# Pooled attention and two dense layers: keys and values of two heads laid out as one run of 144 groups

## The chip, the cores and the metric

One core of a Trainium2 chip runs the whole program. The metric is the time of one execution on the device in microseconds (us). The median of the runs shown is compared, and a profiled execution of the same kernel says where the time lies.

## What is computed

The inputs q, k and v have 8 batches, 8 heads, 576 positions and 64 elements each, in float32. Keys and values are averaged over groups of 8 neighbouring positions, so that a head has 72 pooled keys and 72 pooled values. What follows is the reference, cut to its core:

```
k_p = k.reshape(B, H, Sp, 8, D).mean(axis=3)
v_p = v.reshape(B, H, Sp, 8, D).mean(axis=3)
scores = scale * q @ k_p.T
attn = exp(scores - max(scores)); attn = attn / (sum(attn) + 1e-9)
x = (attn @ v_p) as 4608 tokens x 512
h = x @ w_in;  x = max(0.01 * h, h) @ w_out          # 512 -> 2048 -> 512
h = x @ w_in2; out = max(h, 0) ** 2 @ w_out2         # 512 -> 2048 -> 512
```

## The kernel before

The program runs through three stages that overlap. Attention goes batch by batch and writes its result to a scratch tensor in DRAM; the first layer pair works on the tokens that are ready; from some 500 us on attention is over, and the two layer pairs alone are left. The change lies in attention alone.

**Batch 0** is written out by hand in `first_batch`: a fixed order of loads, pooling, scores, softmax, transposes and output products, mixed with the first weight loads (`fetch`) and their decoding (`w`). `in_order` (L94) ties every instruction of it to the one before on its engine. **Batches 1 to 7** are a generator; the loop over the layer pair's units calls `advance()` to draw a piece of attention between two units, by a count and not by time. In this part the framework orders each engine's work itself, so that an engine may do a piece well before the source's place.

**Loads.** All loads of q, k, v and weights, and the stores of attention, are issued by SyncE (its queue is SPq in the profile) one after the other; only the first half of batch 0's keys goes through ScalarE's queue. A head's 72 groups of 8 positions (a group is one row of 512 values, 2 KB) are cut into 64 and 8. `load_main` (L378, issue on L386) loads the 64: for each of four pairs of heads two transfers of 64 rows (128 KB) each, one to partitions 0 to 63 and one to 64 to 127, so eight for a tensor of a batch. `load_rest` (L392, issue on L395) loads the last 8 groups of all eight heads, 64 rows, in one transfer. Keys and values take turns in the same buffers.

**Keys**, `prepare_k` (L422): `pooled` (L351, instructions on L356) adds the 8 positions of each row in three VectorE steps of 256, 128 and 64 values a row (times the number of pairs). Its last step writes `kd`. In batch 1 TensorE sums instead (`pooled_pe`, L359). The rest's sums go to `rr` and are copied beside themselves (L428). Two TensorE transposes turn `kd` (L440 in batch 0, L448 later), one turns `rr` (L451), all into one PSUM tile `trk`; four ScalarE instructions (L456 and L460, for each half) put the turned keys into `kT`, which is zero elsewhere, so that a matmul yields the scores of two heads at once (L554).

**Values**, `prepare_v` (L464): pooled in the same way into `vd`; two ScalarE and two VectorE instructions (L500, L501), each on 64 partitions, write the high and low parts into `vM`, where a zero block keeps the two heads of a pair apart. The rest's values are multiplied by a block mask on GpSimd (L474), moved by six small SyncE transfers to `rx` (L482), and become `vR`.

**Softmax**, `stage_parts` (L542): for each of 40 chunks of up to 128 tokens VectorE takes the maxima, ScalarE the exponentials (L571) and VectorE the sums' reciprocals (L584). GpSimd multiplies: L586 the first 64 columns of each head (512 values) and twice L593 the last 8 columns of four heads, each three times over (96 values). TensorE transposes the result (L604 and L616), ScalarE and VectorE split it (L605, L606, L617, L619), and `stage_d` multiplies with `vM` and `vR` (L317 to L319 and L638, tile `o`).

PSUM tiles of this part come from `work` (L122), a ring of four banks that transposes, scores, `o` and the layers' `h` share. The core of the parts in question:

```
issue[m // 2].dma_start(out=ts[-1][a * KM:(a + 1) * KM, m % 2],
    in_=src[b, heads[m][a], 0:KM * POOL, :].rearrange("(kk j) d -> kk (j d)", j=POOL))
...
nc.gpsimd.tensor_tensor(
    out=pp[:n, 0:DM].rearrange("p (h x) -> p h x", x=KM), in0=x[:n, :, 0:KM],
    in1=rs[:n].to_broadcast([n, H, KM]), op=ALU.mult)
```

Of the kernel before, what the change touches and what calls it, by code (L numbers as in the profile page):

```python
# [19 lines left out]
KM = 64  # L20
# [7 lines left out]
def raw(ap):  # L28

    return ap.bitcast(F32)  # L30
# [3 lines left out]
def attention_two_mlps(  # L34
# [17 lines left out]
    KR = SP - KM  # L52
    NP = H // 2
    NK = DM // P
    NF = DFF // P
    RG = KR * H // 2
# [265 lines left out]
    def attention():  # L322

        with ExitStack() as s:
# [6 lines left out]

            mask = one.tile([KR * H, H, D], F32, name="mask")
            nc.gpsimd.memset(mask, 1.0 / POOL)
            nc.gpsimd.affine_select(
                out=mask, in_=mask, compare_op=ALU.is_ge, fill=0.0, base=0,
                pattern=[[-KR, H], [0, D]], channel_multiplier=1,
            )
            nc.gpsimd.affine_select(
                out=mask, in_=mask, compare_op=ALU.is_ge, fill=0.0, base=KR - 1,
                pattern=[[KR, H], [0, D]], channel_multiplier=-1,  # L340
# [12 lines left out]
            def pooled(dst, src):  # L353

                for n in (POOL * D // 2, POOL * D // 4, D):
                    nc.vector.tensor_tensor(  # L356
                        out=dst if n == D else src[:, :, 0:n], in0=src[:, :, 0:n], in1=src[:, :, n:2 * n], op=ALU.add
                    )

# [11 lines left out]
            def kv_tile(b, rows, n, name):  # L371

                if b == 0:
                    t = w_late.tile([rows, 2, POOL * D], F32, tag="w", name=name)
                    return t[:, 0:n]
                return kvp.tile([rows, n, POOL * D], F32, tag=f"kv{n}", name=name, bufs=n)

            def load_main(b, src, nm, heads, issue=None):  # L378

                issue = issue or [nc.sync, nc.sync]  # L380
                ts = []
                for m in range(NP):
                    if m % 2 == 0:
                        ts.append(kv_tile(b, P, 2, f"{nm}{b}_{m}"))
                    for a in range(2):
                        issue[m // 2].dma_start(  # L386
                            out=ts[-1][a * KM:(a + 1) * KM, m % 2],
                            in_=src[b, heads[m][a], 0:KM * POOL, :].rearrange("(kk j) d -> kk (j d)", j=POOL),
                        )
                return ts  # L390

            def load_rest(b, src, nm, issue=None):  # L392

                t = kv_tile(b, KR * H, 1, f"r{nm}{b}")
                (issue or nc.sync).dma_start(  # L395
                    out=t[:, 0], in_=src[b, :, KM * POOL:S, :].rearrange("h (kk j) d -> h kk (j d)", j=POOL)
                )
                return t


# [3 lines left out]
            def load_k(b):  # L404
                if b < B:
                    both = [nc.scalar, nc.sync] if b == 0 else [nc.sync, nc.sync]
                    KV["k", b] = (
                        load_rest(b, k, "k", both[1]),
                        load_main(
                            b, k, "k", [[4 * (m // 2) + m % 2 + 2 * a for a in range(2)] for m in range(NP)], both  # L410
                        ),
                    )

            def load_v(b):
                KV["v", b] = (
                    load_rest(b, v, "v"),
                    load_main(b, v, "v", [[2 * m, 2 * m + 1] for m in range(NP)]),
                )

            def prepare_k(b):  # L422
                kr, kk = KV.pop(("k", b))
                i = b % 2
                kd = ap1.tile([P, NP, D], F32, tag="kd", name=f"kd{b}")
                rr = ap1.tile([KR * H, 2, D], F32, tag="rr", name=f"rr{b}")
                pooled(rr[:, 0:1], kr)
                nc.vector.tensor_copy(rr[:, 1], rr[:, 0])  # L428
                if b in K_ON_PE:
                    for ps in pooled_pe(f"kp{b}", kk):  # L430
                        yield
                    nc.scalar.copy(kd, ps)
                else:
                    for m in range(0, NP, 2):
                        pooled(kd[:, m:m + 2], kk[m // 2])
                        if b > 0:
                            yield
                            continue
                        tr = work("trk0") if m == 0 else tr
                        nc.tensor.transpose(  # L440
                            tr[:, m * D:(m + 2) * D], kd[:, m:m + 2].rearrange("p a d -> p (a d)"), ident
                        )
# [4 lines left out]
                for g in range(2 if b > 0 else 0):  # L447
                    nc.tensor.transpose(  # L448
                        tr[:, g * P:(g + 1) * P], kd[:, 2 * g:2 * g + 2].rearrange("p a d -> p (a d)"), ident
                    )  # L450
                nc.tensor.transpose(  # L451
                    tr[:, 2 * P:2 * P + KR * H], rr.rearrange("p a d -> p (a d)"), ident[:KR * H, :KR * H]
                )
                for r in range(2):
                    rows = slice(r * D, (r + 1) * D)
                    nc.scalar.activation(  # L456
                        kT[i][rows, :, r, 0:KM], tr[rows, 0:2 * P].rearrange("p (m x) -> p m x", x=KM),
                        AF.Copy, scale=scale / POOL,
                    )
                    nc.scalar.activation(  # L460
                        kT[i][rows, :, r, KM:SP],
                        tr[rows, 2 * P:2 * P + KR * H].rearrange("p (m r x) -> p m r x", r=2, x=KR)[:, :, r],
                        AF.Copy, scale=scale / POOL,
                    )  # L464
                yield

            def prepare_v(b):
                vr, vv = KV.pop(("v", b))
                if b not in V_ON_PE:
                    vd = ap1.tile([P, NP, D], F32, tag="vd", name=f"vd{b}")  # L470
                rd = ap1.tile([KR * H, 1, D], F32, tag="rd", name=f"rd{b}")
                pooled(rd, vr)
                rv = ap1.tile([KR * H, H, D], F32, tag="rv", name=f"rv{b}")
                nc.gpsimd.tensor_tensor(  # L474
                    out=rv, in0=rd.to_broadcast([KR * H, H, D]), in1=mask, op=ALU.mult
# [22 lines left out]
                for a in range(2):  # L498
                    rows = slice(a * KM, (a + 1) * KM)
                    nc.scalar.activation(vh[rows, :, a], vd[rows], AF.Copy, scale=1.0 / POOL)  # L500
                    nc.vector.scalar_tensor_tensor(  # L501
                        out=vl[rows, :, a], in0=vd[rows], scalar=1.0 / POOL, in1=raw(vh[rows, :, a]),
                        op0=ALU.mult, op1=ALU.subtract,
                    )
# [40 lines left out]
            def stage_parts(b, span, at, off, n):  # L545
# [33 lines left out]
                if b >= EARLY:  # L579
# [5 lines left out]
                pp = xp.tile([P, DM + 6 * RG], F32, tag="p", name=f"p{b}_{at}", bufs=2)  # L585
                nc.gpsimd.tensor_tensor(  # L586
                    out=pp[:n, 0:DM].rearrange("p (h x) -> p h x", x=KM), in0=x[:n, :, 0:KM],
                    in1=rs[:n].to_broadcast([n, H, KM]), op=ALU.mult,
                )
                for g in range(2):  # L590
                    hs = slice(4 * g, 4 * g + 4)
                    o = pp[:n, DM + 3 * g * RG:DM + 3 * (g + 1) * RG].rearrange("p (r h x) -> p r h x", r=3, x=KR)
                    nc.gpsimd.tensor_tensor(  # L593
                        out=o, in0=x[:n, hs, KM:].unsqueeze(1).to_broadcast([n, 3, 4, KR]),
                        in1=rs[:n, hs].unsqueeze(1).to_broadcast([n, 3, 4, KR]), op=ALU.mult,
                    )
# [12 lines left out]

            def rest_part(b, span, at, off, n):  # L610
# [3 lines left out]
                for g in range(2):  # L614
                    c0 = DM + 3 * g * RG
                    nc.tensor.transpose(t2[:3 * RG, g, :n], pp[:n, c0:c0 + 3 * RG], ident[:n, :n])  # L616
# [689 lines left out]
```

## Time and profile before

| | |
|---|---|
| runs shown | 1640.22, 1640.9 and 1642.96 us; median 1640.9 us |
| profiled execution | 1641.07 us, its span 1639.3 us |
| TensorE busy | 1602.6 us, 98% of the span |
| VectorE busy | 1388.1 us, 85% |
| ScalarE busy | 1008.1 us, 61% |
| GpSimd busy | 117.3 us, 7% |
| the chain that ended last, by engine | TensorE 83%, VectorE 8%, ScalarE 4%, DMA 3% |

PE is TensorE's matmuls and PEld its weight loads, which run beside them; DVE is VectorE, ACT ScalarE, POOL GpSimd, SP SyncE. A "q" behind a name is that engine's sequencer, which issues DMAs. L12 is line 12 of the kernel. A span is counted from the first instruction to the last; what lies around it belongs to the execution's time. Busy shares are averages over stages, so a stage is read by itself.

### The profile page before, as it was taken

Reading aid. Unit: us, or ns where it says so; the run is one execution under the profiler, and the core shown is the slowest. Engines: PE = TensorE matmul, PEld = TensorE weight load, DVE = VectorE, ACT = ScalarE, POOL = GpSimd, SP = SyncE. Lnnn points to the kernel's source line nnn. Section 1 sums busy time; section 2 is a strip of 40 time slices with the busy share of each in tenths; the row PEclk is TensorE's granted clock in tenths of the full one; section 3 lists DMA queues with packets and bytes.
Section 4 is the critical chain, followed back from the end, with each engine's and each line's share of the span. In section 5 each row is a group of like instructions: output and inputs, shape, how many; then the busy total and the mean of one; then the engine's idle time right before and its main releaser. Section 6 shows DMA issues by size and latency. Waiting matters only on the chain.

```text
span 1639.3 us, 25990 instructions
## 1 busy us (share of the span) xinstructions
PE 1602.6 (98%) x9032; PEld 1466.8 (89%) x9032; DVE 1388.1 (85%) x2070; ACT 1008.1 (61%) x1930; POOL 117.3 (7%) x149
## 2 busy tenths in 40 slices
PE   5999999999999999999999999999999999999999
PEld 4877788888888999999999999998998998998997
DVE  6899776789889999979759589889789799799687
ACT  6777677755667867667557547456456455465454
POOL 4121222223110000000000000000000000000000
PEclk9999999999999999999999999999999999999999
DMA  8675554777547688887766764865865756756655
GB/s 212 190 203 169 144 134 139 233 217 224 180 157 257 244 284 296 265 304 231 225 190 204 236 186 151 281 196 149 275 187 176 254 177 198 241 171 209 196 167 167
DMA packets 223730, 340.94 MB, mean 208 GB/s; under 512 B 56176, under 2 KB 138096, under 8 KB 223600
## 3 DMA queue, kind: packets, MB, share of 16 engines
q1 hardware_dynamic: 223280, 338.76, 66.3%
q8 instruction: 72, 1.18, 0.3%
q10 hardware_dynamic: 320, 0.52, 0.1%
q14 instruction: 58, 0.48, 0.1%
HBM read 268.44 MB, written 69.21 MB: 206 GB/s over the span
## 4 chain that ended last, share of the span: by engine, by line
PE 83%; DVE 8%; ACT 4%; DMA 3%; issue 1%; SPq 0%; POOL 0%; ACTq 0%; DVEq 0%; POOLq 0%
PE psum L1078 14%; PE psum L317 14%; PE psum L319 14%; PE psum L318 14%; PE psum L1079 7%; PE h L317 3%; PE h L319 3%; PE h L318 3%; PE acc L318 3%; PE acc L319 2%; PE acc L317 2%; PE s L554 1%; ACT x L571 1%; DMA xs<-x 1%; DVE hl_out L245 1%
## 5 line engine op out<-in xcount | busy, mean ns | idle before, releaser
L1078 PE MATMUL psum<-wb_out,oh 128*128 128x512 f32 x1008 | 352.8, 394 | 0.0
L317 PE MATMUL psum<-xh,wb_in 128*128 128x384 f32 x1008 | 337.3, 335 | 2.2 <-ACT s L1052 1.2
L319 PE MATMUL psum<-xh,wb_in 128*128 128x384 f32 x1008 | 336.8, 334 | 0.0
L318 PE MATMUL psum<-xl,wb_in 128*128 128x384 f32 x1008 | 336.8, 334 | 0.0
L930 ACT CAST oh<-g 128x768 fp32r<-128x768 f32 x252 | 210.3, 836 | 160.1 <-PE psum L1078 89.3
L1079 PE MATMUL psum<-wb_out,ol 128*128 128x256 f32 x1008 | 281.8, 280 | 0.0
L931 DVE TENSOR_TENSOR ol<-g,oh 128x768 fp32r<-128x768 f32 x252 | 239.4, 954 | 17.4 <-ACT oh L930 14.9
L1078 PEld LDWEIGHTS psum<-wb_out,oh 128*128 128x128 f32 x1008 | 189.6, 188 | 43.1
L317 PEld LDWEIGHTS psum<-xh,wb_in 128*128 128x128 f32 x1008 | 189.2, 188 | 3.9 <-ACT s L1052 1.5
L318 PEld LDWEIGHTS psum<-xl,wb_in 128*128 128x128 f32 x1008 | 189.2, 188 | 0.2
L319 PEld LDWEIGHTS psum<-xh,wb_in 128*128 128x128 f32 x1008 | 189.2, 188 | 0.0
L1079 PEld LDWEIGHTS psum<-wb_out,ol 128*128 128x128 f32 x1008 | 188.8, 187 | 0.2
L984 ACT CAST wb_in<-wb_in 128x512 fp32r<-128x512 f32 x144 | 89.3, 621 | 146.4 <-DMA wb_in<-ws_in 141.4
L985 DVE TENSOR_TENSOR wb_in<-wb_in 128x512 fp32r<-128x512 f32 x144 | 98.7, 688 | 80.3 <-ACT wb_in L984 79.8
L934 DVE TENSOR_TENSOR g<-g,g 128x768 f32<-128x768 f32 x144 | 136.0, 952 | 1.5 <-ACT g L1006 1.0
L317 PE MATMUL h<-xh,hl_in 128*128 128x512 f32 (+1 forms) x320 | 121.8, 381 | 4.0 <-DVE pt_r L619 2.8
L317 PE MATMUL acc<-gh,hl_out 128*128 128x512 f32 (+1 forms) x320 | 120.2, 382 | 1.4 <-ACT hl_out L244 1.1
L318 PE MATMUL acc<-gl,hl_out 128*128 128x512 f32 (+1 forms) x320 | 118.6, 373 | 0.7 <-DVE gl L865 0.7
L319 PE MATMUL h<-xh,hl_in 128*128 128x512 f32 (+1 forms) x320 | 118.7, 371 | 0.0
L318 PE MATMUL h<-xl,hl_in 128*128 128x512 f32 (+1 forms) x320 | 118.1, 369 | 0.0
L319 PE MATMUL acc<-gh,hl_out 128*128 128x512 f32 (+1 forms) x320 | 117.9, 371 | 0.0
L318 PE MATMUL psum<-ol,wb_out 128*128 128x384 f32 x336 | 112.6, 335 | 0.0
(161 smaller groups left out, 3113.7 us busy)
## 6 DMA issues: line engine op xcount, KB each, us to landing
wb_in<-wd_in SPq DMA_DIRECT2D x108, 512.0 KB
wb_out<-wd_out SPq DMA_DIRECT2D x108, 512.0 KB
wb_in<-ws_in SPq DMA_DIRECT2D x144, 256.0 KB
wb_out<-ws_out SPq DMA_DIRECT2D x144, 256.0 KB
xs<-x SPq DMA_DIRECT2D x18, 768.0 KB
out_dram<-o SPq DMA_DIRECT2D x23, 384.0 KB
q<-in_q_dram SPq DMA_DIRECT2D x32, 256.0 KB
v<-in_v_dram SPq DMA_DIRECT2D x64, 128.0 KB
```

Source lines behind the costliest of these rows:

```text
L245: nc.vector.tensor_tensor(out=lo, in0=w, in1=raw(hi), op=ALU.subtract)
L317: nc.tensor.matmul(outp, ah, bh, start=first, stop=False, **kw)
L318: nc.tensor.matmul(outp, ah, bl, start=False, stop=False, **kw)
L319: nc.tensor.matmul(outp, al, bh, start=False, stop=last, **kw)
L554: nc.tensor.matmul(sc[:n, 2 * m:2 * m + 2].rearrange("p a x -> p (a x)"), qT[:, 2 * e + m, :n], kT[b % 2][:, 2 * e + m].rearrange("p a x - ...
L930: nc.scalar.copy(hi, src)
L931: nc.vector.tensor_tensor(out=lo, in0=src, in1=raw(hi), op=ALU.subtract)
L934: nc.vector.tensor_tensor(out=out_, in0=a, in1=b, op=ALU.subtract)
L984: nc.scalar.copy(whole[:, 0], raw(whole[:, 1]))
L985: nc.vector.tensor_tensor(out=whole[:, 1], in0=raw(whole[:, 1]), in1=raw(whole[:, 0]), op=ALU.subtract)
L1078: nc.tensor.matmul(outp, ah, b, start=first, stop=False, skip_group_check=True)
L1079: nc.tensor.matmul(outp[:, 1], al, b[:, 0], start=False, stop=last, skip_group_check=True)
```

## The change

A pair of heads lies in DRAM as one run of 144 groups. The first 128 now go to the 128 partitions and the other 16 (the second head's last) form the rest, so that the head boundary is at partition 72. Each half of a tensor comes in one transfer of 512 KB, and the rest in one of 128 KB whose outermost index runs over four pairs. The last pooling step of the keys writes every sum twice, four transposes turn them, three ScalarE instructions place them, and the rest gets a PSUM tile of its own; `rr` is one lasting tile whose zero half is never written again. The values' four instructions work on all 128 partitions, with a per-partition factor (`side_of`) that is zero for the other head; `vM` is no longer cleared. GpSimd's main product covers all 72 columns of each head.

```diff
-KM = 64
+    RX = 2 * SP - P
+    RG = NP // 2 * RX
...
-            mask = one.tile([KR * H, H, D], F32, name="mask")
-            nc.gpsimd.memset(mask, 1.0 / POOL)
+            mask = one.tile([NP * RX, NP, 2, D], F32, name="mask")
+            nc.gpsimd.memset(mask[:, :, 0], 0.0)
+            nc.gpsimd.memset(mask[:, :, 1], 1.0 / POOL)
...
+            side_of = one.tile([P, 2], F32, name="side_of")
+            nc.gpsimd.memset(side_of, 1.0 / POOL)
...
+            rr = one.tile([NP * RX, 2, D], F32, name="rr")
+            nc.gpsimd.memset(rr, 0.0)
             for i in range(2):
                 nc.gpsimd.memset(kT[i], 0.0)
-                nc.gpsimd.memset(raw(vM[i]), 0.0)
...
             def pooled(dst, src):
...
+                last = [src[:, :, i * D:(i + 1) * D] for i in range(2)]
+                if len(dst.shape) == 4:
+                    last = [one_of.unsqueeze(2).to_broadcast(list(dst.shape)) for one_of in last]
+                nc.vector.tensor_tensor(out=dst, in0=last[0], in1=last[1], op=ALU.add)
...
-            def load_main(b, src, nm, heads, issue=None):
...
-            def load_rest(b, src, nm, issue=None):
...
+            def load_kv(b, src, nm, issue=None):
+
+                groups = src[b].rearrange("(m a) (kk j) d -> (a kk) m (j d)", a=2, j=POOL)
+                rest = kv_tile(b, NP * RX, 1, f"r{nm}{b}")
+                nc.sync.dma_start(out=rest[:, 0], in_=groups[P:].rearrange("kk m x -> m kk x"))
+                main = []
+                for g in range(2):
+                    main.append(kv_tile(b, P, 2, f"{nm}{b}_{g}"))
+                    (issue or [nc.sync, nc.sync])[g].dma_start(out=main[g], in_=groups[0:P, 2 * g:2 * g + 2])
+                KV[nm, b] = rest, main
...
+            def turned(tr, kd, m):
+                nc.tensor.transpose(tr[:, m * P:(m + 1) * P], kd[:, m].rearrange("p i d -> p (i d)"), ident)
+
+            def put_keys(i, tr, ms):
+
+                for r, at, n in ((0, 0, SP), (1, SP, P - SP)):
+                    rows = slice(r * D, (r + 1) * D)
+                    nc.scalar.activation(
+                        kT[i][rows, ms, r, 0:n],
+                        tr[rows].rearrange("p (m x) -> p m x", x=P)[:, ms, at:at + n],
+                        AF.Copy, scale=scale / POOL,
                     )
 
+            def put_rest(i, b):
+
+                rest = work(f"trr{b}", NP * RX)
+                nc.tensor.transpose(rest, rr.rearrange("p i d -> p (i d)"), ident[:NP * RX, :NP * RX])
+                nc.scalar.activation(
+                    kT[i][D:2 * D, :, 1, P - SP:SP], rest[D:2 * D].rearrange("p (m x) -> p m x", x=RX),
+                    AF.Copy, scale=scale / POOL,
                 )
...
-                kd = ap1.tile([P, NP, D], F32, tag="kd", name=f"kd{b}")
-                rr = ap1.tile([KR * H, 2, D], F32, tag="rr", name=f"rr{b}")
-                pooled(rr[:, 0:1], kr)
-                nc.vector.tensor_copy(rr[:, 1], rr[:, 0])
+                kd = ap1.tile([P, NP, 2, D], F32, tag="kd", name=f"kd{b}")
+                pooled(rr[:, 1:2], kr)
...
+                put_keys(i, tr, slice(0, NP))
+                put_rest(i, b)
                 yield
...
-                    rows = slice(a * KM, (a + 1) * KM)
-                    nc.scalar.activation(vh[rows, :, a], vd[rows], AF.Copy, scale=1.0 / POOL)
+                    own = side_of[:, a:a + 1]
+                    nc.scalar.activation(vh[:, :, a], vd, AF.Copy, scale=own)
...
-                    out=pp[:n, 0:DM].rearrange("p (h x) -> p h x", x=KM), in0=x[:n, :, 0:KM],
-                    in1=rs[:n].to_broadcast([n, H, KM]), op=ALU.mult,
+                    out=pp[:n, 0:H * SP].rearrange("p (h x) -> p h x", x=SP), in0=x[:n],
+                    in1=rs[:n].to_broadcast([n, H, SP]), op=ALU.mult,
...
+                        in0=odd[0][:, ms, P - SP:].unsqueeze(1).to_broadcast([n, 3, 2, RX]),
...
-                    nc.tensor.transpose(t1[:, m, :n], pp[:n, m * P:(m + 1) * P], ident[:n, :n])
+                    nc.tensor.transpose(t1[:, m, :n], pp[:n, 2 * m * SP:2 * m * SP + P], ident[:n, :n])
```

## Rows read from the trace of the kernel before

**Rows 1.** The page: the span, and busy time of TensorE.

```profile
span 1639.3 us, 25990 instructions
...
PE 1602.6 (98%) x9032; PEld 1466.8 (89%) x9032; DVE 1388.1 (85%) x2070; ACT 1008.1 (61%) x1930; POOL 117.3 (7%) x149
```

**Rows 2.** Windows: stretch, length, busy PE, PEld, DVE, ACT, POOL, clock, DMA, GB/s.

```profile
0.00:60.00 60.00, 40.78 (x212) 33.55 (x213) 44.87 (x87) 39.06 (x135) 19.02 (x30) 0.91 0.75 201
60.00:200.00 140.00, 133.02 (x674) 107.74 (x673) 127.38 (x221) 107.70 (x298) 30.13 (x32) 1.00 0.61 178
200.00:500.00 300.00, 296.24 (x1577) 245.34 (x1576) 243.96 (x503) 195.60 (x531) 68.19 (x87) 1.00 0.61 183
500.00:1640.00 1140.00, 1132.60 (x6575) 1080.18 (x6573) 971.91 (x1261) 665.70 (x969) 0.00 (x0) 1.00 0.68 218
```

**Rows 3.** TensorE's waits, 40 to 500 us: total us, times, longest.

```profile
PE pt L604 <- POOL p L586: 2.5, 3, 1.2
```

**Rows 4.** The chain that ended last, in order of time: start, us, what.

```profile
2.66 5.01 DMA k<-in_k_dram
...
8.52 0.44 DVE k L356
...
8.98 0.30 DVE kd L356
...
11.19 0.31 PE trk L451
...
12.66 1.18 PE s L554 x4
...
43.39 0.21 PE o L638
...
43.64 0.63 PE h L317
...
206.64 0.60 ACT g L861
...
256.83 0.59 PE trq L533 x4
```

**Rows 5.** Windows of the first loads, and of the first output products.

```profile
2.00:3.00 1.00, 0.00 (x0) 0.00 (x0) 0.00 (x0) 0.00 (x0) 1.00 (x3) 1.00 0.62 176
3.00:4.00 1.00, 0.00 (x0) 0.00 (x0) 0.00 (x0) 0.69 (x1) 1.00 (x3) 1.00 0.93 305
4.00:5.00 1.00, 0.00 (x0) 0.00 (x0) 0.38 (x1) 0.80 (x2) 0.98 (x3) 1.00 0.94 213
5.00:6.00 1.00, 0.00 (x0) 0.00 (x0) 0.72 (x4) 0.00 (x0) 0.00 (x0) 1.00 0.91 260
6.00:7.00 1.00, 0.00 (x0) 0.00 (x0) 0.00 (x0) 0.00 (x0) 0.00 (x0) 1.00 0.81 215
...
40.00:44.00 4.00, 3.95 (x16) 3.66 (x17) 3.87 (x8) 1.66 (x9) 0.00 (x0) 0.51 0.38 137
```

**Rows 6.** Timeline from 0 to 16 us: start, us, engine, line, operation.

```profile
0.80 2.48 ACTq L386 DMA_DIRECT2D k<-in_k_dram  x4
...
4.62 0.73 DVE L356 TENSOR_TENSOR rk<-rk 64x256 f32<-64x256 f32 x2 [4.62 <-DMA rk<-in_k_dram]
...
8.00 5.02 SPq L386 DMA_DIRECT2D v<-in_v_dram  x8
```

**Rows 7.** Tiles kd, trk and rr: ns min/median/max, first and last start.

```profile
L356 DVE TENSOR_TENSOR kd<-k x14: 275/281/293, 9.0 to 381.8; 128x128 f32<-128x128 f32 x14
...
L448 PE MATMUL trk<-ident,kd x14: 270/272/273, 58.5 to 414.5; 128*128 128x128 f32 x14
...
L428 DVE COPY rr<-rr x8: 176/180/186, 5.6 to 362.9; 64x64 f32<-64x64 f32 x8
```

**Rows 8.** Tile p: GpSimd's main product.

```profile
L586 POOL TENSOR_TENSOR p<-x,rs x40: 1035/1044/1562, 19.2 to 469.5; 128x512 f32<-128x512 f32 x32, 64x512 f32<-64x512 f32 x8
```

**Rows 9.** VectorE's waits, 40 to 500 us: total us, times, longest.

```profile
DVE rv L356 <- DMA rv<-in_v_dram: 2.4, 3, 1.6
```

More of the change, by code (lines that the diff above doesn't have):

```diff
@@ L329, in attention @@
             one = s.enter_context(tc.tile_pool(name="one", bufs=1, side="right"))
-            mask = one.tile([KR * H, H, D], F32, name="mask")
-            nc.gpsimd.memset(mask, 1.0 / POOL)
+            mask = one.tile([NP * RX, NP, 2, D], F32, name="mask")
+            nc.gpsimd.memset(mask[:, :, 0], 0.0)
+            nc.gpsimd.memset(mask[:, :, 1], 1.0 / POOL)
             nc.gpsimd.affine_select(
-                out=mask, in_=mask, compare_op=ALU.is_ge, fill=0.0, base=0,
-                pattern=[[-KR, H], [0, D]], channel_multiplier=1,
+                out=mask[:, :, 1], in_=mask[:, :, 1], compare_op=ALU.is_ge, fill=0.0, base=0,
+                pattern=[[-RX, NP], [0, D]], channel_multiplier=1,
             )
             nc.gpsimd.affine_select(
-                out=mask, in_=mask, compare_op=ALU.is_ge, fill=0.0, base=KR - 1,
-                pattern=[[KR, H], [0, D]], channel_multiplier=-1,
+                out=mask[:, :, 1], in_=mask[:, :, 1], compare_op=ALU.is_ge, fill=0.0, base=RX - 1,
+                pattern=[[RX, NP], [0, D]], channel_multiplier=-1,
+            )
+            side_of = one.tile([P, 2], F32, name="side_of")
+            nc.gpsimd.memset(side_of, 1.0 / POOL)
+            nc.gpsimd.affine_select(
+                out=side_of[:, 0:1], in_=side_of[:, 0:1], compare_op=ALU.is_ge, fill=0.0, base=SP - 1,
+                pattern=[[0, 1]], channel_multiplier=-1,
+            )
+            nc.gpsimd.affine_select(
+                out=side_of[:, 1:2], in_=side_of[:, 1:2], compare_op=ALU.is_ge, fill=0.0, base=-SP,
+                pattern=[[0, 1]], channel_multiplier=1,
             )
@@ L353, in pooled @@
             def pooled(dst, src):
-                for n in (POOL * D // 2, POOL * D // 4, D):
+                for n in (POOL * D // 2, POOL * D // 4):
                     nc.vector.tensor_tensor(
-                        out=dst if n == D else src[:, :, 0:n], in0=src[:, :, 0:n], in1=src[:, :, n:2 * n], op=ALU.add
+                        out=src[:, :, 0:n], in0=src[:, :, 0:n], in1=src[:, :, n:2 * n], op=ALU.add
                     )
+                last = [src[:, :, i * D:(i + 1) * D] for i in range(2)]
+                if len(dst.shape) == 4:
+                    last = [one_of.unsqueeze(2).to_broadcast(list(dst.shape)) for one_of in last]
+                nc.vector.tensor_tensor(out=dst, in0=last[0], in1=last[1], op=ALU.add)
             def pooled_pe(name, src):
@@ L376, in kv_tile @@
                 return kvp.tile([rows, n, POOL * D], F32, tag=f"kv{n}", name=name, bufs=n)
-            def load_main(b, src, nm, heads, issue=None):
[L380 to L390, printed above, removed]
-            def load_rest(b, src, nm, issue=None):
[L394 to L398, printed above, removed]
+            def load_kv(b, src, nm, issue=None):
[7 more added lines that the diff above has]
+                KV[nm, b] = rest, main
             KV = {}
@@ L405, in load_k, with load_v @@
                 if b < B:
[L406 to L411, printed above, removed]
-                    )
[L414 to L417, printed above, removed]
+                    load_kv(b, k, "k", [nc.scalar, nc.sync] if b == 0 else None)
+            def load_v(b):
+                load_kv(b, v, "v")
+            def turned(tr, kd, m):
[7 more added lines that the diff above has]
+                        AF.Copy, scale=scale / POOL,
+                    )
+            def put_rest(i, b):
[4 more added lines that the diff above has]
+                    AF.Copy, scale=scale / POOL,
                 )
@@ L431, in prepare_k @@
                         yield
-                    nc.scalar.copy(kd, ps)
+                    nc.scalar.copy(kd, ps.unsqueeze(2).to_broadcast([P, NP, 2, D]))
                 else:
-                    for m in range(0, NP, 2):
-                        pooled(kd[:, m:m + 2], kk[m // 2])
+                    for g in range(2):
+                        pooled(kd[:, 2 * g:2 * g + 2], kk[g])
                         if b > 0:
@@ L438, in prepare_k @@
                             continue
[L439 to L442, printed above, removed]
+                        tr = work("trk0") if g == 0 else tr
+                        for m in range(2 * g, 2 * g + 2):
+                            turned(tr, kd, m)
                         yield
@@ L446, in prepare_k @@
                     tr = work(f"trk{b}")
[L447 to L464, printed above, removed]
+                    for m in range(NP):
+                        turned(tr, kd, m)
+                put_keys(i, tr, slice(0, NP))
+                put_rest(i, b)
                 yield
@@ L470, in prepare_v @@
                     vd = ap1.tile([P, NP, D], F32, tag="vd", name=f"vd{b}")
-                rd = ap1.tile([KR * H, 1, D], F32, tag="rd", name=f"rd{b}")
+                rd = ap1.tile([NP * RX, 1, D], F32, tag="rd", name=f"rd{b}")
                 pooled(rd, vr)
-                rv = ap1.tile([KR * H, H, D], F32, tag="rv", name=f"rv{b}")
+                rv = ap1.tile([NP * RX, H, D], F32, tag="rv", name=f"rv{b}")
                 nc.gpsimd.tensor_tensor(
-                    out=rv, in0=rd.to_broadcast([KR * H, H, D]), in1=mask, op=ALU.mult
+                    out=rv, in0=rd.to_broadcast([NP * RX, H, D]), in1=mask.rearrange("p m a d -> p (m a) d"),
+                    op=ALU.mult,
                 )
@@ L498, in prepare_v @@
                 for a in range(2):
-                    rows = slice(a * KM, (a + 1) * KM)
-                    nc.scalar.activation(vh[rows, :, a], vd[rows], AF.Copy, scale=1.0 / POOL)
+                    own = side_of[:, a:a + 1]
+                    nc.scalar.activation(vh[:, :, a], vd, AF.Copy, scale=own)
                     nc.vector.scalar_tensor_tensor(
-                        out=vl[rows, :, a], in0=vd[rows], scalar=1.0 / POOL, in1=raw(vh[rows, :, a]),
+                        out=vl[:, :, a], in0=vd, scalar=own, in1=raw(vh[:, :, a]),
                         op0=ALU.mult, op1=ALU.subtract,
@@ L584, in stage_parts @@
                 nc.vector.reciprocal(rs[:n], sm[:n])
-                pp = xp.tile([P, DM + 6 * RG], F32, tag="p", name=f"p{b}_{at}", bufs=2)
+                pp = xp.tile([P, H * SP + 6 * RG], F32, tag="p", name=f"p{b}_{at}", bufs=2)
                 nc.gpsimd.tensor_tensor(
-                    out=pp[:n, 0:DM].rearrange("p (h x) -> p h x", x=KM), in0=x[:n, :, 0:KM],
-                    in1=rs[:n].to_broadcast([n, H, KM]), op=ALU.mult,
+                    out=pp[:n, 0:H * SP].rearrange("p (h x) -> p h x", x=SP), in0=x[:n],
+                    in1=rs[:n].to_broadcast([n, H, SP]), op=ALU.mult,
                 )
+                odd = [t[:n].rearrange("p (m a) x -> p m a x", a=2)[:, :, 1] for t in (x, rs)]
                 for g in range(2):
-                    hs = slice(4 * g, 4 * g + 4)
-                    o = pp[:n, DM + 3 * g * RG:DM + 3 * (g + 1) * RG].rearrange("p (r h x) -> p r h x", r=3, x=KR)
+                    ms = slice(2 * g, 2 * g + 2)
+                    c0 = H * SP + 3 * g * RG
                     nc.gpsimd.tensor_tensor(
-                        out=o, in0=x[:n, hs, KM:].unsqueeze(1).to_broadcast([n, 3, 4, KR]),
-                        in1=rs[:n, hs].unsqueeze(1).to_broadcast([n, 3, 4, KR]), op=ALU.mult,
+                        out=pp[:n, c0:c0 + 3 * RG].rearrange("p (r m x) -> p r m x", r=3, x=RX),
+                        in0=odd[0][:, ms, P - SP:].unsqueeze(1).to_broadcast([n, 3, 2, RX]),
+                        in1=odd[1][:, ms].unsqueeze(1).to_broadcast([n, 3, 2, RX]), op=ALU.mult,
                     )
@@ L614, in rest_part @@
                 for g in range(2):
-                    c0 = DM + 3 * g * RG
+                    c0 = H * SP + 3 * g * RG
                     nc.tensor.transpose(t2[:3 * RG, g, :n], pp[:n, c0:c0 + 3 * RG], ident[:n, :n])
```

2 lines of the change are left out of this document (removed).

## The prediction

> **What bounds the kernel now.** I read the page first: TensorE is busy 1602.6 of 1639.3 us [rows 1], so all that a better order could win back is some 37 us. Then the windows by stage [rows 2]: after 500 us, where the change touches nothing, TensorE idles 7.4 us of 1140. From 200 to 500 us it idles 3.8 of 300, with VectorE at 81% and ScalarE at 65%: TensorE's own work sets the pace there. From 60 to 200 us VectorE is busy 127.4 of 140 and TensorE idles 7.0, so neither alone is the bound. In the first 60 us TensorE is busy only 40.8. That is batch 0, a chain of single steps, and I follow it in the chain of waits [rows 4]: the last piece of batch 0's keys is issued at 2.66 and lands at 7.67, VectorE sums, TensorE turns, the first scores start at 12.66, the last output product ends at 43.60, and the first layer's h starts at 43.64. So a microsecond saved or lost on that chain counts in full unless a later load is not there in time; after 200 us only what TensorE gains or loses counts.
>
> **The change part by part.** The sum is against the profiled execution, 1641.07 us, which stands 0.17 above the median of the runs (1640.9), so the same sum is carried to the median.
>
> *First loads.* Four issues on ScalarE's queue become one. Before, they took from 0.80 to 3.28 and the last began 1.86 us after the first [rows 4, 6]. If issuing were the limit, the keys would come 1.86 us earlier. If the transfers are, hardly at all: the windows from 2 to 7 us moved 176 + 305 + 213 + 260 + 215 = 1169 KB [rows 5], and a batch's keys are 1180 KB. The bounds are 0 and -1.9. Two large transfers queued from the start should hold the rate of the best window, 305 GB/s: 176 KB by 3.0, the other 1004 KB in 3.3 us, so the moving ends near 6.3 instead of 7.0, and I add a tenth for the queue that no longer pauses between issues: **-0.8 us**.
>
> *Batch 0's key path.* The last add writes 256 values a partition instead of 128: 0.44 for 256 [rows 4] against 0.28 to 0.30 for 128 [rows 4, 7], so +0.14 twice on the path. One more transpose per half, a quarter of 0.59 [rows 4], +0.15 for the second half. Against that the key copies no longer wait for the rest's transpose, 0.31 [rows 4], which now goes to a tile of its own. The removed copy of the rest, 0.18 [rows 7], lay beside the keys' load. Four ScalarE copies become three of the same number of values: nothing. GpSimd's setup loses two memsets and gains small ones; it ended before 5.0 us [rows 5], which covers them. Sum **+0.1**.
>
> *GpSimd's product.* L586 takes 576 values instead of 512; a full one takes 1.04 at the median [rows 8], so +0.13, in 40 chunks 5.2 us of an engine that is busy 7% [rows 1]. Bounds 0 and +5.2. L593 keeps its 96 values. TensorE waited for L586 three times from 40 to 500 us [rows 3]: +0.4. In batch 0, of five chunks I count two on the chain: +0.3. Together **+0.7**.
>
> *TensorE.* Batches 1 to 7 turn four blocks instead of two (before, 14 [rows 7]): 14 more at 0.59 / 4 = 0.147 [rows 4], 2.1 us. I put batches 1 and 2 before 200 us, where TensorE has 7.0 us of idle time to hold their 0.6; the other ten are in the stretch in which TensorE is the bound: **+1.5** (bounds 0 and +2.1).
>
> *VectorE later.* Fourteen doubled adds cost 14 x 0.14 = 2.0, eight copies less give 8 x 0.18 = 1.4 [rows 7]. After 200 us TensorE covers it, before it VectorE is the busier: **+0.1**, bounds 0 and +0.6. The values' four instructions have the same 256 values on twice the partitions and a factor per partition; no row shows that form. From below 0; from above the 0.14 that doubled a VectorE add, 28 times (four in each of seven batches), spread on two engines, 2 us each, most of it under TensorE. I take 0, since the count of values a partition is the same, and keep +0.3 for the range.
>
> *SyncE's queue.* Each tensor of a batch has 3 issues instead of 9, 96 fewer in all, 84 of them after batch 0. At 5.02 / 8 = 0.63 us each [rows 6] the queue has 53 us less work by 400 us, and q, weights and stores behind the key loads go out sooner. What that wins is what engines wait for loads: TensorE's waits name no load among the longer ones, VectorE's 2.4 us for the values' rest [rows 9]. Bounds 0 and -2.4; most of it is under TensorE, so **-0.6**. In batch 0 the values' eight issues took 5.02 us for 1 MB, or 209 GB/s, so that load was paced by issuing; in two transfers it is done sooner, and the steps that use it can follow the earlier keys.
>
> *The rest's own PSUM tile.* One more tile per batch from a ring of four banks; whoever takes the bank four allocations later, often h, waits until ScalarE has copied the rest. The trace of before has no such tile. I take 0 and keep up to 0.6 us for each of 7 batches, 4.2, since the wait would be for about one ScalarE instruction of a full bank, 0.60 [rows 4].
>
> Sum: -0.8 + 0.1 + 0.7 + 1.5 + 0.1 - 0.6 = +1.0. On the median that is **1641.9 us**, no change by what can be told, which for this kernel is 0.2% or 3.3 us.
>
> *A rule against the change.* The rest load of batch 0 is issued at 0.80 and VectorE begins on it at 4.62 [rows 6]. Its outermost index ran over eight heads and now runs over four pairs, with the same 64 rows. The Trainium skill, "DMA: Bandwidth & Descriptors", "Why a DMA increments its semaphore by 16 and not by 1", says that a transfer is spread over the largest number of DMA engines up to 16 that divides the slowest dimension of both sides: by it four engines after, eight before. No row here shows which engines carry a load; by that rule the time would be that of the rest-load rival below, without it the forecast's.
>
> **The rivals.**
>
> *Faster: issuing paces batch 0.* Then the keys gain the full 1.9, the values, q and the first weights behind them follow, and the whole chain to 43.64 moves up. In the window 40 to 44 us the granted clock is 0.51 [rows 5], the 1.2 GHz level, after TensorE had stood idle for much of the time before, and an output product takes 0.21 [rows 4]; with less idling these 16 could run at the 2.4 GHz level, up to 16 x 0.11 = 1.8. With the queue's 2.4, and half of TensorE's 1.5 beside stalls, it comes to -1.9 - 1.8 - 2.4 + 0.1 + 0.7 + 0.8 + 0.1 = -4.4, 1636.5 us. For it: the 209 GB/s of the values. Against: the first windows already move 213 to 305 GB/s, and VectorE is busy 44.9 of the first 60 us [rows 2].
>
> *Slower: GpSimd comes to set the transposes.* The product stands between the reciprocals and TensorE's transposes, and GpSimd has 12% more of it. If all 40 chunks are late by 0.13 the sum grows by 5.2 - 0.7 to 1646.4; it is slower by over 0.2% when 18 more chunks than I count are on the path. For it: three waits already. Against: three of 35, and GpSimd mostly idle.
>
> *Slower: the rest load.* If the four pieces take twice as long as the eight, its 3.8 us from issue to use become up to 7.6; in batch 0 that is as late as the keys, and its three adds, 0.9 us, go ahead of theirs in VectorE's order. Later the three waits of rows 9 grow by up to 3 us each. With half of these seen in the time it is 1641.9 + 0.9 + 4.5 = 1647.3, slower than 0.2% when 1.4 us of those waits are seen. Against: VectorE waited for the values' seven later rest loads only three times.
>
> *Slower: the ring of banks*, at 0.6 for each batch, 1646.1 us; it decides from 0.33 a batch on.
>
> That the large transfers land no earlier, as much was in flight before, is the forecast without its first term, 1642.7, and still no change.
>
> **How the numbers follow.** Forecast 0.50, faster 0.27, GpSimd 0.09, the bank 0.08, the rest load 0.06. The forecast's own range, by its bounds, is 1638.5 to 1644. For 8 in 10 I reach to 1635.5 on one side and 1646.5 on the other, which leaves out the rest load's full price and a batch 0 that gains more than counted. Faster by over 0.2%: 0.27; within: 0.50; slower: 0.23.
>
> **What would show it.** Right: the first scores start near 11.9 and h near 43; from 200 to 500 us TensorE's idle time stays below 5 us with ten transposes more; waits for L586 grow to four or five. Wrong: h starts before 41 or after 45; TensorE's waits list the copy of the rest or name L586 ten times or more; VectorE waits more than 5 us for the rest loads; or the stretch after 500 us differs, for which I have no cause.

## The result, and the profile after

The changed kernel is slower: a median of 1658.26 us (4 runs, 1655.71 to 1660.35) against 1640.56 us before (4 runs, 1640.06 to 1642.96), a ratio of 1.0104 [1.0084, 1.0124], or +17.7 us. Measured again later (run e9, below) the same kernel gave 1652.95 against 1641.87 us, 1.0071 [1.0058, 1.0084]. I had forecast 1641.9 and no change; the time lies outside my range. Of the runs below, one execution of e3, at 4081.5 us, is left out of its ratio.

The page of the changed kernel, to be held against [rows 1]:

```profile
span 1658.2 us, 25865 instructions
...
PE 1610.0 (97%) x9048; PEld 1471.1 (89%) x9048; DVE 1389.0 (84%) x2062; ACT 1007.6 (61%) x1922; POOL 124.1 (7%) x152
```

VectorE has 0.9 us more to do, ScalarE 0.5 less, GpSimd 6.8 more and TensorE 7.4 more, while the span grows by 18.9. So 11.5 us of it are idle time of TensorE and 7.4 are work that takes longer. The windows by stage, with the columns of [rows 2], say where:

```profile
0.00:60.00 60.00, 40.55 (x216) 32.91 (x217) 45.23 (x86) 39.56 (x135) 19.00 (x33) 0.89 0.78 206
60.00:200.00 140.00, 129.36 (x635) 104.74 (x636) 124.73 (x208) 103.37 (x286) 33.40 (x29) 0.96 0.57 173
200.00:500.00 300.00, 289.40 (x1548) 238.57 (x1549) 230.71 (x479) 187.82 (x515) 71.73 (x90) 1.00 0.56 170
...
95.00:100.00 5.00, 3.82 (x9) 3.04 (x10) 4.91 (x8) 5.00 (x21) 0.00 (x0) 0.50 0.21 45
95.00:101.80 6.80, 5.62 (x14) 4.35 (x15) 6.55 (x13) 6.25 (x22) 0.60 (x1) 0.50 0.43 131
142.80:146.20 3.40, 3.36 (x10) 2.88 (x11) 3.34 (x5) 3.02 (x4) 2.02 (x2) 0.50 0.02 8
```

TensorE's idle time went from 7.0 to 10.6 us between 60 and 200, and from 3.8 to 10.6 between 200 and 500. VectorE fell from 244.0 to 230.7 busy in the latter, so it stands idle more as well; part of its work has slid behind 500 us. From 95 to 100 us the DMA share is 0.21 and the granted clock 0.50, the 1.2 GHz level. After batch 0 it is 0.50 in two stretches, 6.8 and 3.4 us long; ahead of the first TensorE had stood idle since 92.8 us, ahead of the second twice, for 1.16 and 0.99 us. In the kernel before it is 1.00 from 44 to 1630 us. In the first of them matmuls into `h` start 0.43 us apart:

```profile
96.78 0.63 PE L317 MATMUL h<-xl,hl_in 128*128 128x512 f32 x1
97.20 0.63 PE L318 MATMUL h<-xh,hl_in 128*128 128x512 f32 x1
```

At the full clock they start 0.23 us apart. By these two figures the 9.0 us for which TensorE is busy in the two stretches would have been 4.8, so some 4 us of the loss, an estimate, are the slower clock. The chain that ended last, in order of time, names loads in these places, among others:

```profile
0.80 6.10 DMA rk<-in_k_dram
6.92 0.43 DVE rk L368
...
7.99 0.61 DVE k L368
...
13.11 0.63 PE s L552 x4
...
86.98 6.45 DMA st_in_out<-in_moe_w_out_dram
...
96.18 0.79 PE h L316
...
213.12 5.91 DMA v<-in_v_dram
...
223.58 4.19 DMA rk<-in_k_dram
...
267.81 6.45 DMA rv<-in_v_dram
...
275.59 4.83 DMA rk<-in_k_dram
...
327.80 7.12 DMA rv<-in_v_dram
...
382.10 5.82 DMA rv<-in_v_dram
```

Of its six loads between 200 and 500 us, five are **rest loads** (`rk`, `rv`) of 128 KB, with 4.19 to 7.12 us from issue to landing; in the same stretch the chain of the kernel before names none. Between batch 0 and 200 us the chain names six other loads, four of them weights. In VectorE's waits from 40 to 500 us, where [rows 9] name one load, four stand now (total us, times, longest):

```profile
DVE rk L368 <- DMA rk<-in_k_dram: 4.8, 3, 2.1
DVE rv L368 <- DMA rv<-in_v_dram: 4.2, 3, 3.0
...
DVE v L368 <- DMA v<-in_v_dram: 2.4, 3, 1.1
DVE k L368 <- DMA k<-in_k_dram: 1.7, 1, 1.7
```

That is 13.1 us against 2.4. The next table isn't a view of the profile: I took the starts of all matmuls into tile `h` (the same ones in the same order in every kernel) and list by how many us each comes later than in the kernel before. Each column is one profiled execution; those after the first belong to the experiments.

```
us before   after     e9     e2     e3    e10    e13     e1
   43.6     -1.16  -0.75  -2.69  -2.04  -0.82   1.04   1.10
   85.0      0.36   0.61  -0.27  -0.58  -0.43   1.23   2.90
  115.8      6.33   5.07   3.14   3.97   1.34   2.90   5.49
  206.2      8.12   4.62   2.06   2.89   0.26   4.23   6.34
  274.4     13.21   9.35   5.21   5.29   1.27   4.28   6.62
  337.7     15.68   9.97   5.82   5.15   0.41   3.40   6.62
  386.9     17.78  11.84   7.33   6.78   0.91   3.90   6.58
  504.6     17.74  11.77   7.29   6.96   1.92   4.94   6.16
```

The first h comes 1.16 us sooner; the loss comes in steps between 85 and 390 us and stays at 17.7 from there on.

### The profile page after: what moved, and what is told of

Same layout as the page of the kernel before. It is cut to its first block, busy times and chain, and to the rows that moved or that the text cites. A ratio compares the mean times of both kernels' runs of the same rounds, so it can differ in the third digit from the quotient of the medians.

```text
span 1658.2 us, 25865 instructions
## 1 busy us (share of the span) xinstructions
PE 1610.0 (97%) x9048; PEld 1471.1 (89%) x9048; DVE 1389.0 (84%) x2062; ACT 1007.6 (61%) x1922; POOL 124.1 (7%) x152
## 4 chain that ended last, share of the span: by engine, by line
PE 78%; DVE 9%; DMA 6%; ACT 5%; issue 2%; SPq 0%; POOL 0%; DVEq 0%; ACTq 0%
PE psum L1078 14%; PE psum L316 13%; PE psum L317 13%; PE psum L318 13%; PE psum L1079 7%; PE h L316 2%; PE h L318 2%; PE h L317 2%; PE acc L318 2%; PE acc L317 2%; PE acc L316 2%; ACT x L569 2%; DMA wb_in<-ws_in 2%; DMA st_in_out<-in_moe_w_out_dram 1%; PE s L552 1%
```

## The experiments

My theory after the result: the rest load lands late, since it runs on few DMA engines. The rivals were the wider product, the rest's own tile, the doubled adds and transposes, the large transfers, and the order in which the framework puts each engine's work. Times are medians against the kernel before on the same chip; e5's +2.6, e6's +2.1 and what is called by ratio go by the ratio. e1 to e4 ran on one chip, e5 to e8 on a second, e9 to e12 on a third, e13 and e14 on a fourth, so runs of different groups are compared by ratio; the changed kernel's own ratio differs by 0.33% between the result and e9. In e1, e2, e3, e5, e7, e8 and e13 the bytes or operations are as the edit shows, but from other rows or columns than the computation needs.

**The rest load alone, in both kernels (e1, e2, e3).** e1 puts the changed kernel's rest load into the kernel before, e2 the eight-fold one into the changed kernel, e3 a flat one of 64 rows; the instructions stay in order.

```diff
# e1, in the kernel before
-    in_=src[b, :, KM * POOL:S, :].rearrange("h (kk j) d -> h kk (j d)", j=POOL)
+    in_=src[b].rearrange("(m a) (kk j) d -> (a kk) m (j d)", a=2, j=POOL)[P:].rearrange("kk m x -> m kk x"),
# e2 and e3, in the changed kernel
-    in_=groups[P:].rearrange("kk m x -> m kk x")
# e2
+    in_=src[b, :, S - POOL * POOL:, :].rearrange("h (kk j) d -> h kk (j d)", j=POOL)
# e3
+    in_=groups[P - NP * RX:P, 0]
```

> The kernel before, its rest load alone taken from other rows of the same number: four pieces of 16 rows instead of eight of 8, as in the change; the values are other ones, the order on every engine is that of before. Theory R (the rest load on fewer DMA engines is what costs): most of the 18 us, 1650 to 1658 us, five landing events for a rest load instead of nine, its time from issue to landing 5 to 6 us instead of 4. Theory L (the large transfers land late), theory C (more work in the keys' and GpSimd's steps) and theory O (the framework's changed order): no change, 1640 to 1643 us.

> The kernel after, its rest load alone taken from the rows that it had before, in eight pieces; the values are other ones, the order on every engine is that of after. Theory R: most of the loss goes, 1640 to 1646 us, and VectorE's waits for rk, rv and v fall from 11 us to under 5. Theories L, C and O: no change, 1655 to 1660 us.

> The kernel after, its rest load alone taken from 64 rows in one run, so that its outermost index has 64 entries on both sides; the values are other ones, the order is that of after. Theory R: at least as good as with eight pieces, 1639 to 1645 us, 16 landing events for a rest load. Theories L, C and O: 1655 to 1660 us.

Measured: e1 1646.51 against 1642.51 us, 1.0029 [1.0018, 1.0039]; e2 1647.68, 1.0032 [1.0020, 1.0044]; e3 1647.74, 1.0039 [1.0026, 1.0052]. No theory's range holds any of the three: the rest load's engines (R) matter, by less than R had it. VectorE's waits for `rk`, `rv` and `v` are 5.0 us in e2, 11.4 in the changed kernel. Another table of mine, from the landing events that the trace keeps for each load in the first 500 us (time from issue to the last one, median / longest):

```
kernel   outermost  landing events  rk, us        rv, us
before       8             9        3.86 / 6.59   4.19 / 6.16
after        4             5        4.87 / 6.10   6.20 / 9.20
e1           4             5        5.09 / 7.60   4.73 / 6.70
e2           8             9        3.58 / 5.39   5.00 / 7.69
e3          64            16        3.02 / 4.72   4.73 / 7.54
```

I read the events as one for each DMA engine used and one for those not used: those of the changed kernel's first rest load come at 1.93 us and then, four of them, from 6.11 to 6.90. The Trainium skill, "DMA: Bandwidth & Descriptors", "Why a DMA increments its semaphore by 16 and not by 1", has a transfer spread over the largest number of engines up to 16 that divides the slowest dimension of both sides; 5, 9 and 16 events for 4, 8 and 64 agree with that. The windows of e2 show the same place as after's last row, and the stretch from 200 on:

```profile
200.00:500.00 300.00, 293.13 (x1564) 242.01 (x1563) 237.72 (x488) 192.16 (x519) 69.74 (x87) 1.00 0.58 179
...
95.00:100.00 5.00, 5.00 (x19) 4.03 (x18) 5.00 (x10) 5.00 (x20) 0.41 (x1) 0.69 0.40 136
```

By ratio the four-fold rest load costs the changed kernel 0.72% (1.0104 to 1.0032), some 12 us, or 0.39%, some 6 us, if its ratio is taken from e9, and the kernel before 0.29%, 4.8 us. In e1 the granted clock is 0.50 between 95 and 150 us for as long as in the changed kernel, 10.2 us. Between 206 and 387 us, by the progress table, after's order loses 9.7 us with the rest on four engines, 5.3 on eight and 3.9 on sixteen; the order of before loses 0.2 with it on four (e1). So the price depends on the order of the work around the load as well. What neither edit takes away is about 5 us.

**The wider product (e5, e7).** e5 gives GpSimd's product of the kernel before all 576 columns; e7 is e2 with it cut to 512.

```diff
# e5
-    out=pp[:n, 0:DM].rearrange("p (h x) -> p h x", x=KM), in0=x[:n, :, 0:KM],
+    out=pp[:n, 0:H * SP].rearrange("p (h x) -> p h x", x=SP), in0=x[:n],
```

> The kernel before with GpSimd's product over all 72 columns of each head (576 values instead of 512), the transposes reading other columns of it; the order on every engine is that of before. Of the 5 us that stay with the rest load in eight pieces, theory W (the wider product) expects 2 to 5 here, 1645 to 1648 us beside a before of 1642.5; my forecast's price was 0.7, 1643.2; theories B (the rest's own PSUM tile) and T (doubled adds and two more transposes a batch) expect no change.

> The kernel after with the rest load in eight pieces (other rows) and GpSimd's product over 64 columns of each head again, the transposes reading other columns; the order is that of after. Theory W: 1643 to 1645 us, 2 to 5 under e2_a_rest8. Theories B and T: 1647.7 as there.

Measured: e5 1644.85 against 1641.74, 1.0016 [1.0007, 1.0025], so +2.6; e7 1646.23, 1.0030 [1.0020, 1.0040], level with e2. The product costs 2 to 3 us in the kernel before and nothing that can be told in e2.

**The rest's own tile; single sums (e6, e8).** e6 gives the kernel before a tile of its own for the turned rest; e8 is e2 with each sum written once and two transposes.

```diff
# e6
+    trr = work(f"trr{b}", KR * H)
# e8
-    kd = ap1.tile([P, NP, 2, D], F32, tag="kd", name=f"kd{b}")
+    kd = ap1.tile([P, NP, D], F32, tag="kd", name=f"kd{b}")
```

> The kernel before with the rest's transpose in a PSUM tile of its own, nothing else; the result is the same and the framework orders some of VectorE's and ScalarE's work otherwise. Theory B, the bank or the order that comes with it: 1645 to 1648 us. Theories W and T: 1642.5. My forecast's price: 0.

> The kernel after with the rest load in eight pieces (other rows), the keys' sums written once and two transposes a batch instead of four, the key copies reading them repeatedly; some of VectorE's order changes with it. Theory T: 1643 to 1646 us; my forecast's price was 1.6, so 1646.1. Theories W and B: 1647.7.

Measured: e6 1643.48, 1.0013 [1.0004, 1.0023], +2.1; e8 1644.73, 1.0018 [1.0009, 1.0028], 1.5 us below e7 and, by ratio, 2.3 below e2. The intervals of e7 and e8 overlap. Both edits let the framework order some work anew, so each number is that of the part and the new order together and not the part's price.

**Small pieces, and the kernel again (e4, e9, e10).** e4 loads the rest in four transfers of 16 rows and each half in four of 64 rows; e10 does the former alone; e9 is the changed kernel as it is.

```diff
# e4 and e10
-    nc.sync.dma_start(out=rest[:, 0], in_=groups[P:].rearrange("kk m x -> m kk x"))
+    for m in range(NP):
+        nc.sync.dma_start(out=rest[m * RX:(m + 1) * RX, 0], in_=groups[P:, m])
# e4 only
+    out=main[g][rows, m], in_=groups[rows, 2 * g + m]
```

> The kernel after with the same rows loaded in small transfers: the rest in four of 16 rows, each half in four of 64 rows (128 KB). The computation is that of after; the framework orders some of it otherwise. Theory R or L: 1640 to 1646 us. Theory C (more work): 1655 to 1660 us, as after. Theory O: anything from 1640 to 1660, with TensorE's idle time from 60 to 400 us different and no longer waits for loads.

> The kernel after, unchanged, beside the runs of the same chip as the next three: 1655 to 1660 us, 14 to 18 above before.

> The kernel after, its rest load split into four transfers of 16 rows, each of which can be spread on 16 DMA engines; the large transfers stay and the result is the reference's. Theory R: 1645 to 1648 us, as with the rest in eight pieces, the three further issues a load costing no more than 1 us. If the loss came from the large transfers: 1655 to 1660.

Measured: e4 1647.48 against 1642.51, 1.0031 [1.0020, 1.0043], above the range of R and L; e9 1652.95 against 1641.87, 1.0071; e10 **1643.0** against 1641.87, 1.0004 [0.9994, 1.0013], level with before. Both lie under what I expected. Each piece of e10's rest has 16 landing events and lands in 2.3 (`rk`) or 2.7 us (`rv`) at the median. The rest as a whole, from its first issue to its last landing, takes 4.6 and 5.7 us, not much less than the changed kernel's 4.9 and 6.2. Its windows:

```profile
200.00:500.00 300.00, 296.05 (x1579) 244.90 (x1578) 244.68 (x497) 194.21 (x524) 70.88 (x87) 1.00 0.60 183
...
95.00:100.00 5.00, 5.00 (x27) 4.07 (x26) 5.00 (x10) 4.87 (x21) 0.90 (x1) 1.00 0.56 189
```

TensorE idles 3.95 of 300 us, as before, and the stretch from 95 to 100 is at the full clock. Of VectorE's waits for loads one is left:

```profile
DVE v L368 <- DMA v<-in_v_dram: 1.8, 2, 1.2
```

So the layout, the wider product and the doubled sums can all be had at the time of before, within its interval; what the changed kernel pays for is how it loads, or the order that comes with it. On the same chip e9 and e10 differ by 0.67%, 11 us. From 57 us on e10 also has another order of the engines' work than the changed kernel, e2 and e3 have. In it the values' rest of batch 2 is issued some 30 us sooner; SyncE's timelines in the kernel before, the changed one, e3 and e10:

```profile
95.78 0.65 SPq L395 DMA_DIRECT2D rv<-in_v_dram  x1
...
130.58 0.58 SPq L398 DMA_DIRECT2D rv<-in_v_dram  x1
...
127.63 0.47 SPq L398 DMA_DIRECT2D rv<-in_v_dram  x1
...
100.61 1.72 SPq L399 DMA_DIRECT2D rv<-in_v_dram  x4
```

Whether the 5 us between e3 and e10 are the pieces or the order isn't settled. An early issue alone is not enough: e4 issues this load at 99.07 us and is 1.0031.

**Pieces of other kinds (e13, e14).** e13 is e10, in e10's order on every engine, with every piece on four engines; e14 has the rest on four as in the changed kernel, beside main halves of four pieces.

```diff
# e13
+    out=rest[m * RX:(m + 1) * RX, 0],
+    in_=groups[P + 4 * m:P + 4 * m + 4].rearrange("kk m x -> m kk x"),
# e14
+    out=main[g][rows, m], in_=groups[rows, 2 * g + m]
```

> As e10, four rest transfers of 16 rows and the same order on every engine, but each transfer takes four rows of each of four pairs (the rows arrive in another order, so the values are other ones): outermost index four instead of 16. Theory R alone: 8 to 11 us above e10's 1643, 1651 to 1654, and five landing events for a transfer instead of 16. If what made e10 good was the framework's order: 1643 to 1646.

> The kernel after with its large loads cut into four of 64 rows for each half and the rest load left as it is, on four pairs; the computation and the result are those of after, the framework's order is another one. If the rest load costs by itself, as in e1: 4 to 10 us above e4's 1647.5, 1651 to 1657. If it costs only beside large transfers: 1647.5.

Measured: e13 1644.72 against 1641.71, 1.0021 [1.0010, 1.0032], 2.8 above e10 by ratio (their intervals just touch), though its pieces land only 0.25 us later at the median; e14 1646.24, 1.0028 [1.0017, 1.0039], the same as e4, whose rest ran on 16, though the framework's order is not the same in the two. So the price of the four engines is some 2.8 us here, nothing that can be told beside small main loads, and 6 to 12 in the changed kernel. e13 lies where I expected it if e10's order had made it good, and far under what theory R alone gave: of the 11 us between e9 and e10, some 8 by ratio stay won although the rest runs on four engines again. They belong to the pieces or to the order that comes with them. From 206 to 387 us e13 loses nothing, and none of VectorE's waits from 40 to 500 us is for a rest load.

**Fewer issues alone (e11, e12).** e11 joins pairs of 128 KB loads of the kernel before to 256 KB, e12 in batch 0 only.

```diff
+    out=ts[-1][a * KM:(a + 1) * KM],
+    in_=src[b, h0:h1 + 1:h1 - h0, 0:KM * POOL, :].rearrange("h (kk j) d -> kk h (j d)", j=POOL),
```

> The kernel before with two of its 128 KB loads joined into one of 256 KB, so that a tensor of a batch has four main transfers instead of eight; layout, rest loads and computation are those of before, and the framework orders some VectorE work otherwise. If fewer issues win what they win in batch 0 of e2 (h 2.7 us earlier): 1639 to 1641 us beside a before of 1642. If the framework's changed order costs 1 to 3 us: 1642 to 1645.

> The kernel before with its 128 KB loads joined in pairs in batch 0 alone; the order of all computation is that of before. If issuing paces batch 0, as my rival had it: h starts 1 to 2.7 us before 43.64, and the time falls by as much, 1639.5 to 1641 us beside a before of 1642. If the transfers pace it: no change.

Measured: e11 1644.35 against 1641.87, 1.0015 [1.0006, 1.0024]; e12 1643.35, 1.0012 [1.0003, 1.0021]; the first h comes 2.3 and 1.0 us later. So fewer issues win nothing by themselves, in e12 with the order of before. SyncE's timeline in e12:

```profile
4.49 4.23 SPq L405 DMA_DIRECT2D rv<-in_v_dram  x1
...
14.57 3.69 SPq L191 DMA_DIRECT2D st_in_out<-in_moe_w_in_dram  x1
```

One issue now takes 4.23 us, where the kernel before has 1.58. The queue's time is mostly not saved but spent inside another issue.

## Why the prediction was wrong, by its steps

**First loads (-0.8).** The first h gained 1.16, near the net of this part, but not as I had it. The timeline from 0 to 16 us:

```profile
0.80 0.42 ACTq L402 DMA_DIRECT2D k<-in_k_dram  x1
0.80 0.75 SPq L398 DMA_DIRECT2D rk<-in_k_dram  x1
...
3.40 4.47 SPq L398 DMA_DIRECT2D rv<-in_v_dram  x1
...
6.92 0.73 DVE L368 TENSOR_TENSOR rk<-rk 64x256 f32<-64x256 f32 x2 [6.92 <-DMA rk<-in_k_dram]
...
12.90 2.29 PE L552 MATMUL s<-kT,qT 128*128 128x144 f32 x16
```

The rest lands by 6.92 instead of 4.62 [rows 6], and its adds go ahead of the keys' in VectorE's order, so the first half, landed at 4.34, lies waiting and the scores start at 12.9, not at the 11.9 I looked for. With the rest on eight engines (e2) the scores start at 11.22 and the first h gains 2.69: the step itself was priced too low, and the rest took half of it back.

**Key path, GpSimd, TensorE (+0.1, +0.7, +1.5).** The durations that had rows came out as forecast. The tiles:

```profile
L374 DVE TENSOR_TENSOR kd<-k x14: 409/418/427, 9.1 to 378.8; 128x256 f32<-128x256 f32 x14
...
L415 PE MATMUL trk<-ident,kd x32: 270/272/476, 9.7 to 432.1; 128*128 128x128 f32 x32
...
L584 POOL TENSOR_TENSOR p<-x,rs x40: 1142/1152/1962, 17.9 to 487.1; 128x576 f32<-128x576 f32 x32, 64x576 f32<-64x576 f32 x8
...
L498 ACT ACTIVATE vM<-vd,side_of x14: 492/512/546, 20.0 to 451.1; 128x256 fp32r<-128x256 f32 x14
```

`kd` takes 0.418 us for 0.281 (+0.14, as forecast), the product 1.152 for 1.044 (+0.11; I had +0.13). TensorE's waits from 40 to 500 us name GpSimd twice, three times before [rows 3], where I looked for four or five:

```profile
PE pt L604 <- POOL p L584: 1.4, 2, 1.0
```

The product's cost on the kernel before, 2.6 us (e5), was nevertheless above my 0.7 and inside my bounds of 0 and 5.2. The bank of the rest's own tile, taken at 0, is together with a new order e6's +2.1, inside my 4.2. No run prices the transposes alone; without them and the doubled adds, again in a new order, e8 stands 2.3 us under e2.

**SyncE's queue (-0.6)** failed in its sign. I counted 53 us of issues less as time that later loads gain. In batch 0 `rv`'s issue takes 4.47 us where it took 1.58 before, and the values' last load, issued at 8.42 instead of 12.55 us, lands at 16.09 instead of 15.31. Later, in the new order, the values' rest of batch 2 goes out at 130.58 us instead of 95.78. And joining loads in the kernel before makes it slower (e11, e12).

**The rest load** is the step that failed: the sum had it at nothing. It stood as a rival with a chance of 0.06 at 1647.3, and I argued against it that "VectorE waited for the values' seven later rest loads only three times". That count was of loads on eight engines. On four, and in the same order (e1), VectorE waits five times and 5.8 us for rest loads, where it had waited three times and 2.4 us; in the changed kernel six times and 9.0 us. There `rk` takes 4.87 us at the median instead of 3.86 and `rv` 6.20 instead of 4.19, 1.3 and 1.5 times as long and not twice, and after 200 us, where TensorE sets the pace, TensorE idles 10.6 us instead of 3.8. The rival's mechanism was right; its price, 5.4 us over the forecast, measured 6 to 12 in the changed kernel, 4.8 in the kernel before and 2.8 in e10's order. The price left out what follows a wait: a weight load issued at 86.98 lands 6.45 us later, TensorE idles 3.38 us before the h at 96.18 and then runs at the clock of 0.50. How much of that step is the rest's isn't separated: from 85 to 116 us e3, with the rest on 16 engines, still loses 4.6 of after's 6.0.

The rest of the difference, the 5 us of e2 and e3, is not any one of the other terms: e5 and e6 give 2 to 3 us each when taken alone, yet e10 has both, and the doubled sums, and stands 0.04% above before. The sum had no term for the order in which the framework puts the changed kernel's work. e2 and e3 keep that order and the 5 us, e10 has another and not the 5 us; but no run changes the order alone, so the cause of this share stays open.

## What to carry to other kernels

When a load's shape changes, look at its outermost index on both sides: in the changed kernel 64 rows with four entries outermost landed in 4.9 to 6.2 us at the median, with eight in 3.6 to 5.0, with 64 in 3.0 to 4.7. Splitting the load into pieces with 16 rows outermost, and the order that came with it, took the whole loss away here; the same pieces on four engines took most of it, so measure the split and the spread apart. Price a load by its landing against the moment at which the next engine needs it, not by how often that engine waited before. And look at when a load is issued in the new order, not only at how long it takes. Fewer, larger issues are no gain by themselves if the queue then stands still inside one of them.

## What was not expected of the hardware

- One issue of 128 KB on SyncE's queue took up to 4.47 us when large transfers stood ahead of it (4.23 in e12), against 1.58 for the same load before.
- Of two 512 KB halves started within 1 us, the one on ScalarE's queue landed at 4.34 and the one on SyncE's, behind the rest, at 8.13 us, twelve of its sixteen landing events by 6.92.
- With a factor per partition, and on twice the partitions, ScalarE's instruction on 256 values took 0.512 us instead of 0.416; I had taken nothing. Which of the two costs it, no run separates.
- The same kernel lost 1.04% in the first measurement and 0.71% in the second (e9). Its two largest steps, from 85 to 116 and from 206 to 274 us, are in both profiles (6.0 and 5.1 us, 4.5 and 4.7 in e9), the smaller ones are not; the runs don't say why.
